# Linear attention and a max-out layer on one core: softmax row sums kept and checked on the chip, with a second program part behind a branch

## The chip, the core and the metric

The kernel runs on one core of one Trainium2 chip. The metric is the device time of one execution in microseconds. The kernel before takes 320.04 us (median of 3 runs, 319.87 to 320.14).

## What is computed

Attention with projected keys and values (Linformer), then a layer that takes the elementwise maximum of two products:

```python
k_proj = einsum('ks,bhsd->bhkd', E, k)          # 1024 positions down to 64
v_proj = einsum('ks,bhsd->bhkd', F, v)
scores = q @ k_proj.T / sqrt(64)
scores = scores - max(scores, axis=-1)
attn = exp(scores); attn = attn / (sum(attn, axis=-1) + 1e-9)
x = (attn @ v_proj)  as [8192 tokens, 512]      # 8 batches x 1024 positions, 8 heads x 64
out = maximum(x @ w1, x @ w2) @ w_out           # 512 -> 1024 -> 512, fp32 out
```

The inputs are fp32: q, k and v of 8 x 8 x 1024 x 64, E and F of 64 x 1024, w1 and w2 of 512 x 1024, w_out of 1024 x 512.

## The kernel before

All matmuls are in fp16 with fp32 sums. The kernel does not subtract the row maximum: with a softmax the result is the same as long as no exponential and no sum leaves its number range. The exponentials of the scores are written as fp16 (`ex_sb`). Their row sums are made on TensorE by a product with a matrix of ones (`sums_into`, L353), so each sum stands in 32 partitions at once. ScalarE takes the logarithm of the sums (L382 or L448) into `ld_sb` and then exp(-x) in place (L386, `step_inv`, or L452, `invert`), which gives the inverse sums. VectorE multiplies the attention's output by them (L401, L456).

The max-out layer is rewritten: max(a, b) = b + relu(a - b), so that one product with w1 - w2 (`wd_sb`), a relu and a product with w_out are needed, and a product of x with w2 @ w_out (`m_sb`). These are done by a Strassen-Winograd scheme of 7 products for 8 (`up_steps`, `down_steps`, products p1 to p7), in 16 units of 512 tokens: two for each batch. The matmuls of the up products are at L702, those of the down products at L794. In every unit VectorE adds the parts (L717, L720 for relu, L824 for the output), and ScalarE copies banks out (L676) or makes the output's fourth part (L898). A bank "X" goes on being added to after its first copy: p6 continues on p1's bank.

The order of work is written out by hand. `slots` is one list of steps for all engines: of unit n the down products are slots ("P", n, p, i); between them stand the up products of unit n + 1, slots ("U", n, h, i), where h is the half and i the product; ("G", n, h) is the place where a group of the attention of a later batch (scores, sums, values) is put. `at_slot(key, step)` hangs a step behind a slot. Each engine runs its part of that list in order. So does SP, whose queue carries the first loads, the DMA transposes of q (L317, `step_qt_dma`) and of the projected k (L291), and the stores of the output (L810). GpSimd issues the other loads; for batches 4 and up a small copy on GpSimd (`step_gate`, L297) waits for the transposes before the next batch is loaded.

Buffers come from pools: `soft` (5 buffers) holds `ex_sb` and `ld_sb`; batch 0 takes `ld_sb` from `ppool` instead. `opool` has 14 output tiles; the stores of units 0 and 1 are held back and put into later slots (`held`). Two PSUM tiles named `att_ps` serve the attention. The last unit's last product is cut small (L886, L892), so that the last stores are small. Line L1161 is the end of the program: SP waits for every DMA, and barriers close it.

Of the kernel before, what the change touches and what calls it, by code (L numbers as in the profile page):

```python
# [1 line left out]

# [5 lines left out]

FP32 = mybir.dt.float32
FP16 = mybir.dt.float16  # L10
LN_EXP_SET = 6
ACTF = mybir.ActivationFunctionType
ALU = mybir.AluOpType

# [2 lines left out]
def kernel(  # L17
# [12 lines left out]
    nc = tc.nc  # L30

    B, H, S, D = q.shape
    KP = E.shape[0]
    DM = moe_w1.shape[0]
    DF = moe_w1.shape[1]
    NC = S // 128
# [5 lines left out]

    scale = 1.0 / float(D) ** 0.5

    const = ctx.enter_context(tc.tile_pool(name="const", bufs=1))
    kvq = ctx.enter_context(tc.tile_pool(name="kvq", bufs=4))
    proj = ctx.enter_context(tc.tile_pool(name="proj", bufs=2))
# [1 line left out]
    xpool = ctx.enter_context(tc.tile_pool(name="xpool", bufs=2))  # L49
    gpool = ctx.enter_context(tc.tile_pool(name="gpool", bufs=2))  # L50
    soft = ctx.enter_context(tc.tile_pool(name="soft", bufs=5))
    opool = ctx.enter_context(tc.tile_pool(name="opool", bufs=14))
    ppool = ctx.enter_context(tc.tile_pool(name="ppool", bufs=4))
    ps = ctx.enter_context(tc.tile_pool(name="ps", bufs=1, space=bass.MemoryType.PSUM))

# [9 lines left out]
    def att_banks(dtype=FP32):  # L65
        return ps.tile(
            [128, 2, 512 if dtype == FP32 else 1024], dtype, tag="att", bufs=2, name="att_ps"
        )
# [25 lines left out]
    def alloc(t, n):  # L94
        t[n] = kvq.tile([128, H, NC, D], FP16, tag="kvq", name=f"{n}_sb")

# [22 lines left out]
    w1_sb = big(1).rearrange("p (r f) -> p r f", r=NDC)  # L119
    w2_sb = big(2).rearrange("p (r f) -> p r f", r=NDC)  # L120
    wo_sb = const.tile([128, NFB, DM], FP16, tag="wo", name="wo_sb")
    for g in range(2):
        for w_sb, w in ((w2_sb, moe_w2), (w1_sb, moe_w1)):
            nc.gpsimd.dma_start(
                out=w_sb.rearrange("p (g z) f -> p g z f", z=2)[:, g, :, 0:256],
                in_=w.rearrange("(g p z) f -> p g z f", p=128, z=2)[:, g, :, 0:256],
            )
    for w_sb, w, f0, f1 in (
# [27 lines left out]
    eft = [const.tile([128, NC, KP], FP16, tag=f"eft{i}", name=f"eft{i}") for i in range(2)]  # L156
# [167 lines left out]
    W = HALF // 2  # L324
    Z = D // 2

    def score(t, g, j, banks):
        for h in range(2):
            for o in range(2):
                for e in range(2):  # L330
                    head = 4 * g + 2 * h + e
                    for s in range(2):
                        pos = D * (o ^ e) + s * Z
                        nc.tensor.matmul(  # L334
                            out=banks[e][pos : pos + Z, h * W : (h + 1) * W],
                            lhsT=kpt_of(t, head, o)[:, s * Z : (s + 1) * Z],
                            rhs=t["qt"][o * D : (o + 1) * D, head, j * W : (j + 1) * W],
                            start=True, stop=True,
                        )
        t["ex", g, j] = soft.tile([128, 2, HALF], FP16, tag="soft", name="ex_sb")  # L340
# [24 lines left out]

    def x_out(t, g, j):
        return t["xt"][:, 2 * g : 2 * g + 2, :, j * W : (j + 1) * W]


    def step_sc(t, g, j):  # L370
        sc_ps = att_banks()
        t["ps", g, j] = sc_ps
        score(t, g, j, [sc_ps[:, e, :] for e in range(2)])
        nc.scalar.activation(out=t["ex", g, j], in_=sc_ps, func=ACTF.Exp, scale=scale)  # L374

    def step_dn(t, g, j):
# [4 lines left out]
        t["ld", g, j] = ld  # L381
        nc.scalar.activation(out=t["ld", g, j], in_=dn_ps, func=ACTF.Ln)  # L382

    def step_inv(t, g, j):
        ld = t["ld", g, j]
        nc.scalar.activation(out=ld, in_=ld, func=ACTF.Exp, scale=-1.0)  # L386

    def step_at(t, g, j, att=False, between=None):
        if "xt" not in t:
            new_xt(t)  # L390
        ld = t.pop(("ld", g, j))
        if att:
            both = att_banks()
            at_ps = [both[:, o, :] for o in range(2)]
        else:
            at_ps = [mm_bank() for _ in range(2)]
        values_into(t, g, j, at_ps)
        for o in range(2):
            if o and between is not None:
                between()  # L400
            nc.vector.tensor_tensor(  # L401
                out=x_out(t, g, j)[:, :, o, :],
                in0=at_ps[o].rearrange("q (z n) -> q z n", z=2),
                in1=ld[:, o, None, :].broadcast_to([128, 2, W]),
                op=ALU.mult,
            )
# [18 lines left out]
    def scores(t, g, j, banks):  # L425
        for e in t["first"]:
            nc.scalar.activation(  # L427
                out=t["ex", g, j][:, e, :], in_=banks[e], func=ACTF.Exp, scale=scale
            )
# [7 lines left out]
    def step_da(t, g, j, between, ln_later):  # L437
        if "xt" not in t:
            new_xt(t)
        dn_ps = att_banks()[:, :, 0:W]  # L440
        at_ps = att_banks()
        sums_into(t, g, j, dn_ps)
        values_into(t, g, j, [at_ps[:, o, :] for o in range(2)])
        between()
        ld = soft.tile([128, 2, W], FP32, tag="soft", name="ld_sb")

        def ln():
            nc.scalar.activation(out=ld, in_=dn_ps, func=ACTF.Ln)  # L448
            return invert

        def invert():
            nc.scalar.activation(out=ld, in_=ld, func=ACTF.Exp, scale=-1.0)  # L452
            return finish

        def finish():
            nc.vector.tensor_tensor(  # L456
                out=x_out(t, g, j).rearrange("q z o n -> q o z n"),
                in0=at_ps.rearrange("q o (z n) -> q o z n", z=2),
                in1=ld[:, :, None, :].broadcast_to([128, 2, 2, W]),
                op=ALU.mult,  # L460
            )

        return ln if ln_later else ln()
# [503 lines left out]
    f = lambda s, *a: lambda: s(tiles[0], *a)  # L967
# [56 lines left out]
    def at_slot(key, s, *a):  # L1024
        steps.setdefault(key, []).append(lambda: s(*a))
# [14 lines left out]
    for n, x in enumerate((  # L1040
# [4 lines left out]
        for name in x.split():  # L1045
# [6 lines left out]
            else:  # L1052
                g, j = int(name[2]), int(name[3])
# [22 lines left out]
    for b in range(3, B):  # L1076
        t = tiles[b]
        n = 2 * b - 3
# [13 lines left out]
    for i, (new, old) in enumerate(zip([*groups[1:], none], groups)):  # L1092
        n, h = divmod(i + 2, 2)
# [9 lines left out]
    for n, (b, o) in enumerate(units):  # L1103
# [14 lines left out]
        if n:  # L1118
            end = ("U", n - 1, 1, 6) if n > 1 else ("P", 0, 6, 1)
            m = 0 if n == last else 2  # L1120
            one = end if n == 1 else ("G", n, 0) if n in kv_units else ("P", n, 0, 0)
            for key, i in (end, 0), (one, 1), (("P", n, 1, m), 2), (("P", n, 2, m), 3):
                at_slot(key, sums_g, u, (i,))

    pending = []
    for key, slot in slots:
        r = slot()
        pending = [g for g in [r, *(f() for f in pending)] if g is not None]
        for s in steps.pop(key, ()):
            r = s()  # L1130
# [2 lines left out]
    assert not pending  # L1133
    assert not steps
    assert not held


# [28 lines left out]
```

## Time and profile before

| | |
|---|---|
| median of 3 runs | 320.04 us (319.87 to 320.14) |
| profiled execution, span | 318.0 us |
| outside the span, against the median | 2.0 us |
| instructions in the span | 9177 |
| TensorE busy | 312.1 us |
| VectorE busy | 240.4 us |
| ScalarE busy | 206.1 us |
| GpSimd busy | 40.0 us |
| DMA | 53.41 MB in 76424 packets |

The profile is of one execution on the chip. Its own time is the span, from the first to the last instruction, and the time around it that belongs to the launch. Engines are named PE (TensorE matmul), PEld (TensorE weight load), DVE (VectorE), ACT (ScalarE), POOL (GpSimd) and SP (SyncE); a q behind a name means its sequencer, which issues DMAs and waits for semaphores. In a timeline the columns are the start in us, the length in us, the engine, the line, the operation with its tiles and shapes, and in brackets the idle time before and what ended it. In a list by line the numbers are count, shortest/median/longest duration in ns, and first and last start.

### The profile page before, as it was taken

Reading aid. Unit: us, or ns where it says so; the run is one execution under the profiler, and the core shown is the slowest. Engines: PE = TensorE matmul, PEld = TensorE weight load, DVE = VectorE, ACT = ScalarE, POOL = GpSimd, SP = SyncE. Lnnn points to the kernel's source line nnn. Section 1 sums busy time; section 2 is a strip of 40 time slices with the busy share of each in tenths; the row PEclk is TensorE's granted clock in tenths of the full one; section 3 lists DMA queues with packets and bytes.
Section 4 is the critical chain, followed back from the end, with each engine's and each line's share of the span. In section 5 each row is a group of like instructions: output and inputs, shape, how many; then the busy total and the mean of one; then the engine's idle time right before and its main releaser. Section 6 shows DMA issues by size and latency. Waiting matters only on the chain.

```text
span 318.0 us, 9177 instructions
## 1 busy us (share of the span) xinstructions
PE 312.1 (98%) x3920; PEld 253.5 (80%) x3920; DVE 240.4 (76%) x437; ACT 206.1 (65%) x372; POOL 40.0 (13%) x63
## 2 busy tenths in 40 slices
PE   8989999999999999999999999999999999999996
PEld 3555588788887888788887888788887888888885
DVE  2366888877969696996969696996969696969683
ACT  2476843777776777477776778477776777765541
POOL 8269002003000300030000400040000000000000
DMA  7999999999969899899989999989969131303124
GB/s 184 203 200 197 204 206 203 207 180 157 205 119 197 152 217 245 212 182 172 237 196 213 165 200 244 221 154 179 235 142 207 45 102 35 101 33 102 35 99 132
DMA packets 76424, 53.41 MB, mean 168 GB/s; under 512 B 29536, under 2 KB 76000, under 8 KB 76384
## 3 DMA queue, kind: packets, MB, share of 16 engines
q0 software_dynamic: 30688, 28.05, 56.4%
q1 hardware_dynamic: 45408, 24.58, 32.2%
q8 instruction: 30, 0.49, 0.6%
q10 hardware_dynamic: 288, 0.20, 0.2%
q14 instruction: 10, 0.08, 0.1%
HBM read 57.15 MB, written 16.78 MB: 233 GB/s over the span
## 4 chain that ended last, share of the span: by engine, by line
PE 92%; DMA 4%; POOL 1%; ACT 1%; DVE 0%; issue 0%; POOLq 0%; DVEq 0%
PE mm_ps L794 47%; PE mm_ps L702 27%; PE mm_ps L481 4%; DMA v_sb<-in_v_dram 4%; PE att_ps L346 3%; PE mm_ps L189 3%; PE mm_ps L334 2%; PE mm_ps L590 2%; PE att_ps L231 1%; PE mm_ps L305 1%; POOL k_sb L102 0%; POOL q_sb L102 0%; ACT ld_sb L382 0%; ACT ex_sb L374 0%; DVE o_sb L892 0%; PE att_ps L513 0%
## 5 line engine op out<-in xcount | busy, mean ns | idle before, releaser
L676 ACT COPY p_sb<-mm_ps 128x512 f32<-128x512 f32 x179 | 101.8, 592 | 49.4 <-PE mm_ps L702 27.6
L794 PEld LDWEIGHTS <-big 128*128 128x128 f16 x768 | 73.6, 98 | 11.8 <-issue 3.6
L794 PE MATMUL mm_ps<-T_sb,big 128*128 128x256 f16 x576 | 76.9, 273 | 0.0
L717 DVE TENSOR_TENSOR gt_sb<-mm_ps,p_sb 128x512 f16<-128x512 f32 x56 | 38.5, 688 | 43.9 <-PE mm_ps L702 43.6
L702 PE MATMUL mm_ps<-big,big 128*128 128x256 f16 x336 | 50.4, 273 | 0.0
L702 PEld LDWEIGHTS <-big 128*128 128x128 f16 x448 | 43.8, 98 | 5.1
L794 PE MATMUL mm_ps<-wo_sb,gt_sb 128*128 128x256 f16 x256 | 42.6, 273 | 0.0
L794 PEld LDWEIGHTS <-gt_sb 128*128 128x128 f16 x376 | 35.7, 98 | 6.7 <-issue 2.7
L427 ACT ACTIVATE ex_sb<-mm_ps 128x512 f16<-128x512 f32 x50 | 27.2, 596 | 18.0 <-PE mm_ps L334 12.3
L702 PEld LDWEIGHTS <-wd_sb 128*128 128x128 f16 x336 | 32.9, 98 | 3.8
L702 PE MATMUL mm_ps<-xt_sb,wd_sb 128*128 128x256 f16 x224 | 32.8, 273 | 0.0
L456 DVE TENSOR_TENSOR xt_sb<-att_ps,ld_sb 128x1024 f16<-128x1024 f32 x26 | 31.7, 1219 | 0.2
L794 PE MATMUL mm_ps<-m_sb,xt_sb 128*128 128x256 f16 x128 | 24.4, 273 | 0.0
L824 DVE TENSOR_TENSOR o_sb<-mm_ps,p_sb 128x512 f32<-128x512 f32 x32 | 21.9, 683 | 2.8 <-ACT p_sb L853 2.0
L297 POOL COPY junk<-qt_sb 1x1 f16<-1x1 f16 x6 | 1.5, 246 | 175.1 <-DMA qt_sb<-q_sb 175.1
L720 DVE TENSOR_SCALAR gt_sb<-gt_sb 128x512 f16<-128x512 f16 (+1 forms) x60 | 21.5, 359 | 2.1
L662 DVE TENSOR_TENSOR big<-gt_sb 128x1024 f16<-128x1024 f16 x32 | 21.9, 683 | 0.0
L794 PE MATMUL mm_ps<-wo_sb,big 128*128 128x256 f16 x128 | 21.5, 273 | 0.0
L763 ACT ACTIVATE gt_sb<-mm_ps 128x512 f16<-128x512 f32 x28 | 16.8, 601 | 5.7 <-PE mm_ps L702 5.7
L794 PE MATMUL mm_ps<-T_sb,gt_sb 128*128 128x256 f16 x120 | 20.3, 273 | 0.0
L794 PEld LDWEIGHTS <-xt_sb 128*128 128x128 f16 x188 | 18.3, 98 | 2.3 <-issue 0.2
L717 DVE TENSOR_TENSOR gt_sb<-p_sb 128x512 f16<-128x512 f32 x28 | 19.1, 682 | 0.6 <-ACT p_sb L676 0.6
(113 smaller groups left out, 432.3 us busy)
## 6 DMA issues: line engine op xcount, KB each, us to landing
out_dram<-o_sb SPq DMA_DIRECT2D x62, 256.0 KB, 2.7
k_sb<-in_k_dram POOLq DMA_DIRECT2D x7, 1024.0 KB, 10.6
v_sb<-in_v_dram POOLq DMA_DIRECT2D x7, 1024.0 KB, 16.6
q_sb<-in_q_dram POOLq DMA_DIRECT2D x5, 1024.0 KB, 23.5
q_sb<-in_q_dram POOLq DMA_DIRECT2D x6, 512.0 KB, 16.2
big<-in_moe_w_dram POOLq DMA_DIRECT2D x12, 128.0 KB, 6.6
v_sb<-in_v_dram POOLq DMA_DIRECT2D x4, 256.0 KB, 13.5
wo_sb<-in_moe_w_out_dram POOLq DMA_DIRECT2D x1, 1024.0 KB, 10.8
```

The lines of the kernel that those rows point to most:

```text
L189: nc.tensor.matmul(out=kv_ps[r * KP : (r + 1) * KP, h * D : (h + nh) * D], lhsT=eft[i][:, c, :], rhs=t[w][:, h0 + h : h0 + h + nh, c, :], ...
L427: nc.scalar.activation(out=t["ex", g, j][:, e, :], in_=banks[e], func=ACTF.Exp, scale=scale)
L456: nc.vector.tensor_tensor(out=x_out(t, g, j).rearrange("q z o n -> q o z n"), in0=at_ps.rearrange("q o (z n) -> q o z n", z=2), in1=ld[:, ...
L481: nc.tensor.matmul(out=h_ps, lhsT=wd_sb[:, r, fb * 128 : (fb + 1) * 128], rhs=t["xt"][:, r, :, j * W : (j + 1) * W], start=(r == 0), stop= ...
L662: nc.vector.tensor_tensor(out=S(i), in0=S(0) if x is None else x, in1=y(), op=op)
L676: copy(out=x, in_=bank)
L702: nc.tensor.matmul(out=bank[:, m * W : (m + 1) * W], lhsT=w_[:, n_, (2 * d + m) * 128 : (2 * d + m + 1) * 128], rhs=a[:, n_, :], start=(n ...
L717: nc.vector.tensor_tensor(out=c_blk(j, c), in0=two(x), in1=two(y), op=ALU.add)
L720: nc.vector.tensor_scalar_max(ap, ap, 0.0)
L763: nc.scalar.activation(out=out, in_=in_, func=ACTF.Relu)
L794: nc.tensor.matmul(out=bank[i][:, 0:CH] if two_banks else bank[:, i * CH : (i + 1) * CH], lhsT=a(c)[:, i * 128 : (i + 1) * 128], rhs=w_(c) ...
L824: nc.vector.tensor_tensor(out=o_sb, in0=two(x), in1=two(y), op=ALU.add)
```

## The change

Each inverse (`step_inv`, `invert`) is followed by a small DMA on SP's queue: 4 of the 128 rows (one out of every 32 equal ones), 512 values each, go into a tile `checked` of 128 x 512. There are 32 such DMAs, and after the last one `checked` holds every row's inverse sum. In the half ("U", 14, 1) VectorE takes the largest and the smallest value of each partition (on the bits as integers, which orders positive floats and also catches what is not a number), compares them with 1/16 and 1/60000, and writes 0, 1 or 2 to `bad`. A matmul with ones adds `bad` over the partitions, and ScalarE copies one element to `flag`. At the end of the program every engine loads `flag` and branches: where it is not zero, `tile_shifted` computes the whole output again in fp32, with row maxima subtracted. The code marks a place for a branch hint in the same half. The output pool has 13 tiles in place of 14, which makes room for the new tiles.

```diff
+SUM_MIN, SUM_MAX = 16.0, 60000.0
...
+    guard = ctx.enter_context(tc.tile_pool(name="guard", bufs=1))
+    flag = guard.tile([1, 1], I32, name="flag")
+    outer, ctx = ctx, ExitStack()
...
-    opool = ctx.enter_context(tc.tile_pool(name="opool", bufs=14))
+    opool = ctx.enter_context(tc.tile_pool(name="opool", bufs=13))
...
+    checked = const.tile([128, 2 * W], FP32, name="checked")
+    n_checked = [0]
+
+    def check(inv):
+        rows = checked[4 * n_checked[0] : 4 * n_checked[0] + 4, :]
+        n_checked[0] += 1
+        nc.sync.dma_start(
+            out=rows, in_=inv.rearrange("(a z) o w -> a z (o w)", z=Z)[:, 0, :]
+        )
+
+    def step_guard():
+        bits = checked.bitcast(I32)
+        ends = const.tile([128, 4], FP32, name="ends")
+        bad = ends.bitcast(FP16)[:, 4:5]
+        as_bits = lambda x: float(struct.unpack("i", struct.pack("f", x))[0])
+        for i, op in enumerate((ALU.max, ALU.min)):
+            nc.vector.tensor_reduce(
+                out=ends[:, i : i + 1], in_=bits, op=op, axis=mybir.AxisListType.X
+            )
+        nc.vector.tensor_scalar(
+            out=ends[:, 0:1], in0=ends[:, 0:1], scalar1=as_bits(1.0 / SUM_MIN), scalar2=None,
+            op0=ALU.is_gt, op1=ALU.bypass,
+        )
+        nc.vector.tensor_scalar(
+            out=bad, in0=ends[:, 1:2], scalar1=as_bits(1.0 / SUM_MAX), scalar2=ends[:, 0:1],
+            op0=ALU.is_lt, op1=ALU.add,
+        )
+        return bad
+
+    def step_flag(bad):
+        n_ps = att_banks()[:, 0, 0:1]
+        nc.tensor.matmul(out=n_ps, lhsT=ones16[:, 0:128], rhs=bad, start=True, stop=True)
+        nc.scalar.copy(out=flag, in_=n_ps[0:1, :])
+
     def step_inv(t, g, j):
         ld = t["ld", g, j]
         nc.scalar.activation(out=ld, in_=ld, func=ACTF.Exp, scale=-1.0)
+        check(ld)
...
         def invert():
             nc.scalar.activation(out=ld, in_=ld, func=ACTF.Exp, scale=-1.0)
+            check(ld)
             return finish
...
+    bad = []
+    at_slot(("U", last - 1, 1, 0), lambda: bad.append(step_guard()))
+    at_slot(("U", last - 1, 1, 1), lambda: step_flag(bad[0]))
+    at_slot(("U", last - 1, 1, 1), lambda: tc.mark_branch_hint_location(
+        "shifted", "LikelyTaken", mybir.ALL_ENGINES))
...
+    ctx.close()
+
+    with tc.If(nc.values_load(flag, min_val=0, max_val=256, ...), preferred_fallthrough_block=True, label="shifted"):
+        tile_shifted(tc, q, k, v, E, F, moe_w1, moe_w2, moe_w_out, out)
+
+
+@with_exitstack
+def tile_shifted(ctx, tc, q, k, v, E, F, w1, w2, w_out, out):
...
+    for b in range(B):
+        body(b)
```

`tile_shifted` is unrolled: for each of the 8 batches it loads k, v and q in fp32, projects them, and for each 128 positions makes the scores, subtracts the row maximum, and does the softmax, the two up products, their maximum and the down product, without overlap between steps. `preferred_fallthrough_block=True` puts its instructions right behind the branch, so that the branch is taken, over them, where the flag is zero.

More of the change, by code (lines that the diff above doesn't have):

```diff
@@ L1 @@
+import struct
 from contextlib import ExitStack
@@ L10 @@
 FP16 = mybir.dt.float16
+I32 = mybir.dt.int32
 LN_EXP_SET = 6
+SUM_MIN, SUM_MAX = 16.0, 60000.0
 ACTF = mybir.ActivationFunctionType
@@ L382, in step_dn @@
         nc.scalar.activation(out=t["ld", g, j], in_=dn_ps, func=ACTF.Ln)
+    checked = const.tile([128, 2 * W], FP32, name="checked")
[7 more added lines that the diff above has]
+    def step_guard():
+        assert n_checked[0] == B * H * S // (2 * W) // 4
+        bits = checked.bitcast(I32)
[19 more added lines that the diff above has]
+        nc.scalar.copy(out=flag, in_=n_ps[0:1, :])
     def step_inv(t, g, j):
@@ L1135, with bank, turned, body @@
     assert not held
+    ctx.close()
+    with tc.If(nc.values_load(flag, min_val=0, max_val=256, skip_runtime_bounds_check_because="it is only compared with zero"), preferred_fallthrough_block=True, label="shifted"):
+        tile_shifted(tc, q, k, v, E, F, moe_w1, moe_w2, moe_w_out, out)
+@with_exitstack
+def tile_shifted(ctx, tc, q, k, v, E, F, w1, w2, w_out, out):
+    nc = tc.nc
+    B, H, S, D = q.shape
+    KP, DM, DF = E.shape[0], *w1.shape
+    P = 128
+    NC, NX, NG = S // P, DM // P, DF // P
+    AX = mybir.AxisListType.X
+    once = ctx.enter_context(tc.tile_pool(name="once", bufs=1))
+    work = ctx.enter_context(tc.tile_pool(name="work", bufs=1))
+    psum = ctx.enter_context(tc.tile_pool(name="psum", bufs=1, space=bass.MemoryType.PSUM))
+    ident = once.tile([P, P], FP32, name="ident_s")
+    make_identity(nc, ident)
+    def bank(n):
+        return psum.tile([P, 512], FP32, tag=f"b{n}", name=f"b{n}")
+    def turned(dst, blocks, n):
+        cols, rows = blocks[0].shape
+        for i0 in range(0, len(blocks), 512 // cols):
+            part = blocks[i0 : i0 + 512 // cols]
+            ps = bank(n)
+            for i, x in enumerate(part):
+                nc.tensor.transpose(
+                    out=ps[0:rows, i * cols : (i + 1) * cols], in_=x, identity=ident[0:cols, 0:cols]
+                )
+            nc.vector.tensor_copy(
+                out=dst[0:rows, i0 * cols : (i0 + len(part)) * cols], in_=ps[0:rows, 0 : len(part) * cols]
+            )
+    w1_sb, w2_sb = (once.tile([P, NX, DF], FP32, name=f"w{i}_s") for i in (1, 2))
+    wo_sb = once.tile([P, NG, DM], FP32, name="wo_s")
+    for sb, w in (w1_sb, w1), (w2_sb, w2), (wo_sb, w_out):
+        nc.gpsimd.dma_start(out=sb, in_=w.rearrange("(r p) f -> p r f", p=P))
+    ef = once.tile([KP, 2, S], FP32, name="ef_s")
+    eft = once.tile([P, 2, NC * KP], FP32, name="eft_s")
+    for i, w in enumerate((E, F)):
+        nc.gpsimd.dma_start(out=ef[:, i], in_=w)
+        turned(eft[:, i], [ef[:, i, c * P : (c + 1) * P] for c in range(NC)], 0)
+    def body(b):
+        x_in = {}
+        for n, src in (("k", k), ("v", v), ("q", q)):
+            x_in[n] = work.tile([P, NC, H, D], FP32, tag="in" if n != "q" else "q", name=f"{n}_s")
+            for h in range(H):
+                nc.gpsimd.dma_start(
+                    out=x_in[n][:, :, h, :], in_=src[b, h].rearrange("(c p) d -> p c d", p=P)
+                )
+            if n == "q":
+                break
+            proj = work.tile([KP, H * D], FP32, tag=f"{n}p", name=f"{n}p_s")
+            ps = bank(1)
+            for c in range(NC):
+                nc.tensor.matmul(
+                    out=ps[0:KP, :], lhsT=eft[:, "kv".index(n), c * KP : (c + 1) * KP],
+                    rhs=x_in[n][:, c].rearrange("p h d -> p (h d)"),
+                    start=(c == 0), stop=(c == NC - 1),
+                )
+            nc.vector.tensor_copy(out=proj, in_=ps[0:KP, :])
+            x_in[n + "p"] = proj
+        kpt = work.tile([D, H * KP], FP32, tag="kpt", name="kpt_s")
+        turned(kpt, [x_in["kp"][:, h * D : (h + 1) * D] for h in range(H)], 0)
+        for c in range(NC):
+            qt = work.tile([D, H * P], FP32, tag="qt", name="qt_s")
+            turned(qt, [x_in["q"][:, c, h, :] for h in range(H)], 0)
+            sc_ps = bank(1)
+            for h in range(H):
+                nc.tensor.matmul(
+                    out=sc_ps[:, h * KP : (h + 1) * KP], lhsT=qt[:, h * P : (h + 1) * P],
+                    rhs=kpt[:, h * KP : (h + 1) * KP], start=True, stop=True,
+                )
+            sc = work.tile([P, H, KP], FP32, tag="sc", name="sc_s")
+            top = work.tile([P, H], FP32, tag="top", name="top_s")
+            per = lambda a: a[:, :, None].broadcast_to([P, H, KP])
+            nc.vector.tensor_copy(out=sc.rearrange("p h k -> p (h k)"), in_=sc_ps)
+            nc.vector.tensor_reduce(out=top, in_=sc, op=ALU.max, axis=AX)
+            nc.vector.tensor_tensor(out=sc, in0=sc, in1=per(top), op=ALU.subtract)
+            nc.scalar.activation(out=sc, in_=sc, func=ACTF.Exp, scale=1.0 / float(D) ** 0.5)
+            nc.vector.tensor_reduce(out=top, in_=sc, op=ALU.add, axis=AX)
+            nc.vector.tensor_scalar(
+                out=top, in0=top, scalar1=1e-9, scalar2=None, op0=ALU.add, op1=ALU.bypass
+            )
+            nc.vector.reciprocal(out=top, in_=top)
+            nc.vector.tensor_tensor(out=sc, in0=sc, in1=per(top), op=ALU.mult)
+            at = work.tile([KP, H * P], FP32, tag="at", name="at_s")
+            turned(at, [sc[:, h, :] for h in range(H)], 0)
+            x_ps = bank(1)
+            for h in range(H):
+                nc.tensor.matmul(
+                    out=x_ps[:, h * D : (h + 1) * D], lhsT=at[:, h * P : (h + 1) * P],
+                    rhs=x_in["vp"][:, h * D : (h + 1) * D], start=True, stop=True,
+                )
+            x = work.tile([P, DM], FP32, tag="x", name="x_s")
+            nc.vector.tensor_copy(out=x, in_=x_ps)
+            xt = work.tile([P, DM], FP32, tag="xt", name="xt_s")
+            turned(xt, [x[:, r * P : (r + 1) * P] for r in range(NX)], 0)
+            g = work.tile([P, DF], FP32, tag="g", name="g_s")
+            for f in range(0, DF, 512):
+                for i, w in enumerate((w1_sb, w2_sb)):
+                    ps = bank(2 + i)
+                    for r in range(NX):
+                        nc.tensor.matmul(
+                            out=ps, lhsT=xt[:, r * P : (r + 1) * P], rhs=w[:, r, f : f + 512],
+                            start=(r == 0), stop=(r == NX - 1),
+                        )
+                    if i == 0:
+                        nc.vector.tensor_copy(out=g[:, f : f + 512], in_=ps)
+                    else:
+                        nc.vector.tensor_tensor(
+                            out=g[:, f : f + 512], in0=g[:, f : f + 512], in1=ps, op=ALU.max
+                        )
+            gt = work.tile([P, DF], FP32, tag="gt", name="gt_s")
+            turned(gt, [g[:, r * P : (r + 1) * P] for r in range(NG)], 0)
+            o_ps = bank(1)
+            for r in range(NG):
+                nc.tensor.matmul(
+                    out=o_ps, lhsT=gt[:, r * P : (r + 1) * P], rhs=wo_sb[:, r, :],
+                    start=(r == 0), stop=(r == NG - 1),
+                )
+            o_sb = work.tile([P, DM], FP32, tag="o", name="o_s")
+            nc.vector.tensor_copy(out=o_sb, in_=o_ps)
+            nc.gpsimd.dma_start(
+                out=out.rearrange("(n c p) m -> n c p m", c=NC, p=P)[b, c], in_=o_sb
+            )
+    for b in range(B):
+        body(b)
```

## The prediction

> **What bounds the kernel now.** I read the page first: how busy each engine is, the instruction queues, and the shares of the chain that ended last.
>
> ```profile
> span 318.0 us, 9177 instructions
> PE 312.1 (98%) x3920; PEld 253.5 (80%) x3920; DVE 240.4 (76%) x437; ACT 206.1 (65%) x372; POOL 40.0 (13%) x63
> q8 instruction: 30, 0.49, 0.6%
> q14 instruction: 10, 0.08, 0.1%
> PE 92%; DMA 4%; POOL 1%; ACT 1%; DVE 0%; issue 0%; POOLq 0%; DVEq 0%
> ```
>
> TensorE is the bound: it is busy 98% of the span, and the chain is TensorE for 92%. So work on another engine costs nothing unless TensorE, or the end of the program, comes to wait for it. The two queue rows are the program itself being read: 30 blocks of 0.49 MB / 30 = 16 KB, which at 7,840 TensorE instructions (3920 + 3920) is TensorE's own stream at about 62 bytes each, and 10 blocks of 8 KB for other engines.
>
> Next, the timeline where the change puts its new VectorE work and its one new matmul (unit 14, second half), VectorE and TensorE together.
>
> ```profile
> 298.45 0.29 DVE L720 TENSOR_SCALAR gt_sb<-gt_sb 128x512 f16<-128x512 f16 x1
> 300.73 0.60 PE L702 MATMUL mm_ps<-xt_sb,wd_sb 128*128 128x256 f16 x4
> 301.17 0.38 PE L794 MATMUL mm_ps<-m_sb,big 128*128 128x256 f16 x2
> 301.44 0.69 DVE L717 TENSOR_TENSOR gt_sb<-mm_ps,p_sb 128x512 f16<-128x512 f32 x1 [2.70 <-PE mm_ps L702]
> 302.30 0.59 ACT L676 COPY p_sb<-mm_ps 128x512 f32<-128x512 f32 x1 [1.17 <-PE mm_ps L702]
> ```
>
> VectorE ends the second relu of p3 at 298.74 and stands idle 2.70 us until p2's product; ScalarE stands idle 1.17 us just behind. Matmuls start 0.109 us apart (four in 0.44).
>
> Then the tail: the last links of the chain, and what the closing line L1161 does on each queue.
>
> ```profile
> 305.70 7.86 PE mm_ps L794 x72
> 313.56 0.67 PE mm_ps L886 x6
> 314.31 0.90 DVE o_sb L892 x3
> ...
> L1161 SPq EVENT_SEMAPHORE  x11: 17/28/28, 315.6 to 317.9; - x11
> L1161 SPq DRAIN  x3: 7/7/13, 317.1 to 317.4; - x3
> L1161 PEldq DRAIN  x2: 13/615/1217, 313.7 to 317.5; - x2
> L1161 DVEq DRAIN  x2: 19/174/330, 314.9 to 317.5; - x2
> L1161 ACTq DRAIN  x2: 8/79/150, 315.3 to 317.4; - x2
> ```
>
> The sequencers come to the end at 313.7 (TensorE, running ahead of its matmuls), 314.9 (VectorE), 315.3 (ScalarE) and 315.6 (SP). All then stand until 317.1, when the last store (issued at 315.24) has landed and SP may drain. So there is room of 3.4, 2.2, 1.8 and 1.5 us in which an end of program can hide. The last 0.9 us, to 318.0, are the closing barriers.
>
> Last, the early stretch, where SP's queue is tight.
>
> ```profile
> 59.76 0.63 ACT L386 ACTIVATE ld_sb<-ld_sb 128x512 f32<-128x512 f32 x1
> 66.01 6.18 SPq L317 DMA_TRANSPOSE qt_sb<-q_sb  x2
> 72.88 1.09 ACT L427 ACTIVATE ex_sb<-mm_ps 128x512 f16<-128x512 f32 x2 [0.65 <-PE mm_ps L334]
> ```
>
> SP waits 63.5 us for q of batch 2 before the first transpose (the queue's own waits), and the inverse sums of batch 1 are made in that wait.
>
> **The changed order.** I compared the order of instructions of both kernels on every engine. TensorE, VectorE, ScalarE and GpSimd keep their order. They gain only: a weight load and a 128x1 matmul; two reductions and two 128x1 operations; one 1x1 copy; and on every engine a prefetch hint, a register load and a branch. The hint stands first in the program, not in unit 14 where the code marks it. SP gains 32 DMAs, four for a batch, in between stores and transposes.
>
> **32 row copies (8 KB each).** SP issues a DMA in 0.34 to 0.58 us, so 32 cost some 15 us of a queue that waits 163.7 us for VectorE's sums alone. Queued behind each waiting copy are the stores and transposes made after it, but the inverse it waits for precedes theirs, so they lose at most 0.6 us. Stores have a median landing of 2.7 us; a buffer of ex or ld is taken again two groups (some 18 us) later. The bytes are 0.26 of 53.4 MB. The one tight place is 66 to 73 us: copies 5 and 6 (batch 1) now sit between the two transposes. The first transpose is not moved; it ends at about 66.0 + 3.1 = 69.1, copy 5 is issued by 69.7 and, landing behind the transpose's data (GpSimd saw those at 71.68), is there at about 72. The exponential that takes its buffer starts at 72.88. So 0 now, 0.9 us of cover, and if that is gone up to 1 us. The second transpose goes 1.2 us later; its scores come at 80.63 and the loads behind it (batch 3) are used from 97 us on: hidden. 0 in the sum.
>
> **Extra waits.** ScalarE gets 18 more semaphore instructions, VectorE 6, at 17 to 28 ns: 0.6 us beside TensorE's work: 0.
>
> **Output buffers 14 to 13.** Followed through, the closest reuse now is the 19th tile on the store of the 6th issue, some 510 program positions earlier; at 9115 positions in 318 us that is 17 us against a landing of 2.7 us plus up to 6.2 us behind two transposes: 0.
>
> **Reductions and flag.** A 128x512 f32 operation takes 0.68 us (683 ns, L824), a small one at most 0.23 (227 ns, L153): 2 x 0.68 + 2 x 0.23 = 1.8 us, from 298.74 to 300.6, inside the 2.70 us and ahead of the flag's matmul at 301.17. Were a reduction as slow as the 1.22 us of L456, it would be 2.9 us, and TensorE would wait 0.5 us. I take 0. The 1x1 copy (0.22 us, L239) fits into ScalarE's 1.17 us. On TensorE the new pair costs 0.055 (the spacing of the 128-column pairs in the tail, six in 0.33 us) to 0.109 us: +0.1.
>
> **Hint at the start.** A sequencer instruction: 0.02 to 0.5 us (a semaphore row, a DMA issue); on the path, as the start waits for loads that SP and GpSimd issue: +0.1.
>
> **The end.** Every engine now loads the flag into a register, compares and jumps over the second part. No trace of before shows a register load: it lies between a semaphore instruction (0.03) and a whole DMA (1.7 us, the 64 KB store); I take 0.6, near the 0.58 of SP's first DMA issue, also one request to memory by a sequencer. [...] Branch and jump: 0.1.
>
> What decides is whether the target is there. It lies 1 instruction beyond the branch for SP, 136 for ScalarE (8.5 KB, about the next block), 1503 for VectorE (94 KB) and 4711 for TensorE (0.29 MB, 18 blocks). The rows show blocks streamed one after another, so I expect VectorE and TensorE to have the second part's blocks, not the target's. A fetch costs the block's own transfer, 0.6% x 16 x 318 / 30 = 1.0 us for TensorE and 0.1% x 16 x 318 / 10 = 0.5 us for the others, plus the fixed part of a small DMA, 1.7 us as the 64 KB store: 2.7 and 2.2. Bounds: 1.0 (the transfer alone) and 3.7 us (the 256 KB load of E).
> - SP: 315.6 + 0.7, then its semaphores, still before 317.1.
> - VectorE: 314.9 + 0.7 + 2.2 + 0.1 = 317.9, 0.8 past 317.1.
> - TensorE: 313.7 + 0.7 + 2.7 + 0.1 = 317.2.
> - ScalarE: if it too misses, 318.3, 1.2 past.
> - GpSimd ends its work at 246.4 and branches once the flag is written, at about 302: nothing.
>
> I take VectorE's 0.8 us plus 0.1 for a part of ScalarE's: +0.9. [...]
>
> **Sum.** 0.1 + 0.1 + 0.9 = +1.1 us on a span of 318.0, so 319.1. The median of the runs, 320.04, is 2.0 above the span, and nothing in the change touches what lies around it: 321.1 us. The runs spread by 0.27 us; 0.2%, or 0.64 us, is about what a measurement of this kernel can tell from no change.
>
> **Rivals.**
> 1. Not slower: the hint works. The target's block is fetched ahead, VectorE is through at 315.7 and SP at 316.6 with its dozen semaphores (0.3 us), both before 317.1. Left are the 0.2 us of pair and hint: 320.2. The point is a fetch of 317.1 - 315.7 = 1.4 us; below it nothing shows. For it: the instruction is made for this branch, and so far ahead that there is time. Against: it stands some 315 us and up to 30 blocks before its branch, so what it fetches may long be overwritten.
> 2. The early copies: copy 5 lands after 72.9, ScalarE's exponential and the copies behind it slip, and TensorE, which adds to a bank only three products (1.3 us) after the one that is copied out, waits. Price up to 1 us there, besides the 1.1: 322.1. Against: 0.9 us of cover.
> 3. The long fetch: 3.7 us on ScalarE and VectorE, 315.3 + 0.7 + 3.7 + 0.1 = 319.8, 2.7 us past: 322.9.
> 4. The check misfires and the second part runs. Sums of 64 exponentials of small scores lie near 64, in range, so the flag is zero. If not, thousands of fp32 matmuls would at least double the time.
>
> **How the numbers follow.** Forecast 0.50, rival 1 0.33, rival 2 0.06, rival 3 0.08, rival 4 0.01; 0.02 for a schedule that happens to fall better. Short fetches (under 1.8 us) leave a tenth of the forecast's chance within 0.2%, and a fifth of rival 1's ends above it. Slower: 0.45 + 0.07 + 0.06 + 0.08 + 0.01 = 0.67; same 0.05 + 0.26 = 0.31; faster 0.02. The range reaches from rival 1 to rival 3: 320.1 to 322.9.
>
> **What would show it.** Right: TensorE's chain unchanged to about 314.5, VectorE's hole filled from 298.7, no wait at the 128x1 matmul, and VectorE's and perhaps ScalarE's first instruction behind the branch 2 us or more after it, with SP waiting for that and not for the store. Wrong: the closing drain still at about 1.5 us after SP's last issue; or TensorE idle near 73 or 301 us; or a late start.

## The result, and the profile after

The changed kernel takes 322.13 us (median of 4 runs, 321.98 to 322.76), the kernel before beside it 320.06 us (4 runs, 319.87 to 320.14). The ratio is 1.0066, with a 95% interval of 1.0051 to 1.008: slower by 2.07 us, where 1.1 had been forecast.

The page of after, the lines that answer to those of before:

```profile
span 320.4 us, 9299 instructions
PE 311.9 (97%) x3921; PEld 253.6 (79%) x3921; DVE 241.2 (75%) x441; ACT 206.2 (64%) x373; POOL 40.3 (13%) x63
q8 instruction: 31, 0.51, 0.6%
q14 instruction: 13, 0.11, 0.1%
PE 91%; DMA 4%; POOL 1%; ACT 1%; issue 1%; DVE 0%; POOLq 0%; DVEq 0%
```

TensorE is busy for the same time. The two queue rows are the program itself being read: one more block of TensorE (q8, 31 for 30) and three more of other engines (q14, 13 for 10). That is the first hint of where to look.

The place of the check, in the timeline of after, VectorE, TensorE and ScalarE:

```profile
298.93 0.29 DVE L763 TENSOR_SCALAR gt_sb<-gt_sb 128x512 f16<-128x512 f16 x1
299.23 1.28 DVE L407 TENSOR_REDUCE ends<-checked 128x1 f32<-128x512 int32 x2
301.64 0.17 PE L422 MATMUL att_ps<-ends,ones 128*128 128x1 f16 x1
301.88 0.15 ACT L423 CAST flag<-att_ps 1x1 int32<-1x1 f32 x1 [0.27 <-PE att_ps L422]
301.91 0.69 DVE L760 TENSOR_TENSOR gt_sb<-mm_ps,p_sb 128x512 f16<-128x512 f32 x1 [1.09 <-PE att_ps L422]
```

The hole that VectorE had here is filled, and 1.09 us of it is left. No wait stands in front of the 128x1 matmul. The row of VectorE names that matmul as its releaser, but the product it adds ended in the same moment, and the length of the idle time adds up as before: 2.70 less the 1.6 us of new work.

The end of the chain, then the jump (L1187: register load and branch on every engine), then the closing line, which is L1345 now:

```profile
306.20 7.86 PE mm_ps L837 x72
314.06 0.67 PE mm_ps L929 x6
314.81 0.91 DVE o_sb L935 x3
```
```profile
L1187 PEldq TENSOR_LOAD <-flag x1: 805/805/805, 314.2 to 314.2; - x1
L1187 PEldq COMPARE_BRANCH  x1: 385/385/385, 315.1 to 315.1; - x1
L1187 DVEq TENSOR_LOAD <-flag x1: 574/574/574, 315.4 to 315.4; - x1
L1187 DVEq COMPARE_BRANCH  x1: 84/84/84, 316.1 to 316.1; - x1
L1187 ACTq COMPARE_BRANCH  x1: 68/68/68, 316.6 to 316.6; - x1
L1187 SPq COMPARE_BRANCH  x1: 72/72/72, 316.8 to 316.8; - x1
```
```profile
L1345 SPq EVENT_SEMAPHORE  x14: 17/28/28, 317.0 to 320.4; - x14
L1345 SPq DRAIN  x3: 7/7/13, 319.6 to 319.9; - x3
L1345 PEldq DRAIN  x2: 8/8/8, 315.7 to 319.9; - x2
L1345 DVEq DRAIN  x2: 10/14/17, 316.8 to 319.9; - x2
L1345 ACTq DRAIN  x2: 8/8/8, 317.2 to 319.9; - x2
```

All engines are past the jump and at the closing line at 315.7 (TensorE), 316.8 (VectorE), 317.2 (ScalarE) and 317.0 us (SP). Nobody stands at a branch. Yet SP drains only at 319.6, where it drained at 317.1 before. What SP waits for is the stores: its last one is issued at 315.74 and is complete at 319.41, 3.67 us later (the completion is the last count on the store's semaphore in the trace). In the trace of before it is issued at 315.24 and complete at 316.98, 1.74 us later. So the 2.49 us by which the span grew (320.44 less 317.95) are 0.50 us of a chain that ends later (314.81 against 314.31 for VectorE's last link), 1.93 us of a store that lands later, and 0.06 us in the closing barriers.

The landing itself can be taken apart. Each store is counted in 16 parts. Of the last three, 15 parts are there at 317.16, 317.34 and 317.50, and one part of each at 318.94, 319.21 and 319.41. The DMA view of two windows shows what moved then (queue q1 is SP's, q10 ScalarE's, q8 and q14 the program's own). In the trace of before, 315.9 to 317.7 us has no block:

```profile
q1 hardware_dynamic: 201, 0.11, 20.3%
q10 hardware_dynamic: 144, 0.07, 13.1%
```

In the trace of after, the same window has three:

```profile
DMA packets 459, 0.31 MB, mean 175 GB/s; under 512 B 61, under 2 KB 456, under 8 KB 456
q8 instruction: 1, 0.02, 5.2%
q14 instruction: 2, 0.02, 3.5%
```

And then, in the trace of after, 317.72 to 319.6 us:

```profile
DMA packets 26, 0.02 MB, mean 8 GB/s; under 512 B 3, under 2 KB 26, under 8 KB 26
q1 hardware_dynamic: 17, 0.01, 3.1%
q10 hardware_dynamic: 9, 0.00, 0.7%
```

The second window holds 26 packets, 9 of them on q10, which is a sixteenth of the 144 packets of ScalarE's store: it looks as if one DMA engine out of 16 is late. In the first window lie one block of 16 KB for TensorE (from 316.17 us, 1.51 us long) and two of 8 KB for other engines (from 317.28 and 317.68, 0.53 and 0.47 us). So a new explanation offers itself, which the forecast did not have: **the jump makes the sequencers read program at the very moment at which the last stores move, and the blocks stand in front of one engine's share of them.** The profile does not name the DMA engine of a packet; that block and late packets share one is inferred from the sixteenth and from the times. The times are close: the first packet of the late share starts at 317.66 us, just as TensorE's block ends (316.17 and 1.51, so 317.68), and it is the same in the runs below (317.61 and 317.62 in e14_block_away, 317.71 and 317.73 in e9_near_hint).

### The profile page after: what moved, and what is told of

It is laid out like the page before. It is cut to its first block, busy times and chain, and to the rows that moved or that the text cites. A ratio compares the mean times of both kernels' runs of the same rounds, so it can differ in the third digit from the quotient of the medians.

```text
span 320.4 us, 9299 instructions
## 1 busy us (share of the span) xinstructions
PE 311.9 (97%) x3921; PEld 253.6 (79%) x3921; DVE 241.2 (75%) x441; ACT 206.2 (64%) x373; POOL 40.3 (13%) x63
## 4 chain that ended last, share of the span: by engine, by line
PE 91%; DMA 4%; POOL 1%; ACT 1%; issue 1%; DVE 0%; POOLq 0%; DVEq 0%
PE mm_ps L837 46%; PE mm_ps L745 27%; PE mm_ps L524 4%; DMA v_sb<-in_v_dram 4%; PE att_ps L352 3%; PE mm_ps L195 3%; PE mm_ps L340 2%; PE mm_ps L633 2%; PE att_ps L237 1%; PE mm_ps L311 1%; POOL q_sb L108 0%; ACT ld_sb L388 0%; ACT ex_sb L380 0%; DVE o_sb L935 0%; PE att_ps L556 0%
```

## The experiments

Each figure is the median, with the ratio to the kernel before run beside it. "Block" is the start of TensorE's program block near the end, "landed" the last part of the last store, "drain" SP's first drain at the closing line, all from the profiled execution.

| kernel | median us | ratio, 95% | block | landed | drain |
|---|---|---|---|---|---|
| before | 320.06 | | none | 316.98 | 317.12 |
| after | 322.13 | 1.0066 (1.0051 to 1.008) | 316.17 | 319.41 | 319.55 |
| e1_no_branch | 320.0 | 0.9992 (0.9974 to 1.001) | none | 317.40 | 317.54 |
| e3_no_hint | 321.72 | 1.0054 (1.0035 to 1.0073) | 316.3, 319.5 | 318.79 | 319.00 |
| e2_near | 322.12 | 1.0065 (1.0042 to 1.0088) | 316.2 | 318.81 | 318.95 |
| e8_near_plain | 320.51 | 1.0011 (1.0002 to 1.0021) | none | 317.36 | 317.66 |
| e9_near_hint | 322.49 | 1.0077 (1.006 to 1.0094) | 316.02 | 319.35 | 319.49 |
| e6_early_load | 321.7 | 1.0055 (1.0039 to 1.0071) | 315.7 | 318.56 | 318.70 |
| e10_early_plain | 321.79 | 1.0056 (1.0036 to 1.0076) | 315.1, 318.4 | 318.42 | 318.56 |
| e7_late_jump | 321.19 | 1.0028 (1.0013 to 1.0043) | 318.8 | 317.51 | 318.46 |
| e11_hint_te | 322.13 | 1.0071 (1.0054 to 1.0088) | 315.92 | 318.94 | 319.08 |
| e12_hint_others | 322.19 | 1.0071 (1.0054 to 1.0088) | 316.18 | 319.15 | 319.30 |
| e13_hint_two | 322.22 | 1.0089 (1.0052 to 1.0126) | 318.6 | 321.80 | 321.94 |
| e14_block_away | 322.18 | 1.0069 (1.0052 to 1.0086) | 316.01 | 319.25 | 319.40 |

### The check without the jump: e1_no_branch

The hint, the register load, the branch and the second part are left out; copies, reductions and flag stay.

```diff
-    at_slot(("U", last - 1, 1, 1), lambda: tc.mark_branch_hint_location(
-        "shifted", "LikelyTaken", mybir.ALL_ENGINES))
...
-    with tc.If(nc.values_load(flag, ...), ...):
-        tile_shifted(tc, q, k, v, E, F, moe_w1, moe_w2, moe_w_out, out)
```

> The change without its end: the sums are still kept, reduced and turned into the flag, but nothing loads the flag, there is no hint, no branch and no second part. Theory A (after the jump the sequencers fetch the program block behind the target, and that fetch stands in front of one DMA engine's sixteenth of the last stores): the last stores land within 1.8 us of their issue as before, 320.1 to 320.6 us. Theory B (register load, compare, jump and a longer list of closing waits make the end longer): the same 320.1 to 320.6. Theory C (0.4 us of the loss come from the hint at the start): no shift of TensorE at 40 us, 320.1; if the shift stays, it is the copies or chance, 320.5.

It is as fast as before. Everything that the check does on the chip is hidden, and the whole loss belongs to what this run leaves out: the hint, the register load, the jump and the second part. Its last VectorE link starts at 314.71 us, 0.40 later than in the trace of before, without a loss in the median. So most of the 0.50 us by which the chain of after is shifted is likely the chance of single profiled executions, and not the change. The shift is there within the first 40 us, where TensorE still waits for the first loads.

### Without the hint: e3_no_hint

```diff
-    at_slot(("U", last - 1, 1, 1), lambda: tc.mark_branch_hint_location(
-        "shifted", "LikelyTaken", mybir.ALL_ENGINES))
```

> The whole change without the branch hint. Theory A: the hint had the target block there in time; without it TensorE, VectorE and ScalarE wait 1 to 2.7 us for a block after the compare, and the block behind follows, so SP's closing wait ends 1 to 3 us later than with the hint: 322.5 to 325 us. Theory B, or a hint without effect: 322.1 us. Theory C: 0.4 us less from the start in either case.

It is not slower than with the hint: 321.72 us, below the 322.5 to 325 us of Theory A. The 0.4 us less than with the hint are Theory C's figure, but the first matmul starts only 0.10 us sooner (1.45 against 1.55 us), and the intervals of the two kernels overlap. The long wait comes, though, at TensorE's branch:

```profile
L1185 PEldq COMPARE_BRANCH  x1: 4189/4189/4189, 314.6 to 314.6; - x1
```

4.19 us for a branch that takes 0.385 us with the hint. So with the hint TensorE does not stand at its branch; but without it TensorE is through at 318.8 us, just when the last store lands, which is late here too (318.79).

### A short second part: e2_near, e8_near_plain, e9_near_hint

First the second part was cut to one DMA (128 rows of the output over 128 others; it does not compute the output where the flag is set), with the hint kept:

```diff
-        tile_shifted(tc, q, k, v, E, F, moe_w1, moe_w2, moe_w_out, out)
+        nc.gpsimd.dma_start(out=out[0:128], in_=out[128:256])
```

> The whole change, with hint, register load, compare and jump on all engines, but the second part is one DMA, so that the target lies one to three instructions beyond the branch. Theory A: no block is fetched at the end, the last stores land in time, 320.1 to 320.6 us. Theory B: the same end as with the long second part, 321.6 to 322.1 us.

The time is the one of Theory B, and a block is read (at 316.2 us), which Theory A did not expect. But this does not decide: the schedule put SP's last store behind the branch (issued at 316.96 for 315.74 us), which alone makes the end later. In the next pair the DMA touches all rows, so that every store stays ahead of the branch as in the changed kernel; one is without the hint, one with it:

```diff
+        nc.gpsimd.dma_start(out=out[0:4096], in_=out[4096:8192])
```

> As the near second part before, but that part now copies half of the output onto the other half, so that all stores stay ahead of the branch, and there is no hint. Theory A (the instruction blocks that are fetched after the jump stand in front of the last stores on one DMA engine): the branch stays in a block that is there, nothing is fetched, the last stores land 1.8 us after issue: 320.0 to 320.4 us. Theory B (load, compare, jumps and the longer list of closing waits cost by themselves): 321.5 to 322.1.

> The same with the hint. Theory A, with the hint replacing the next block by the target's: one 16 KB block for TensorE is still fetched right after its jump, though the target is two instructions away, and the last stores of one DMA engine land 1 to 1.5 us late: 321.0 to 321.8 us. A hint that does nothing for a near target: 320.0 to 320.4. Theory B: 321.5 to 322.1, as without hint.

Without the hint (L1185 is the jump, L1212 the closing line):

```profile
L1185 PEldq TENSOR_LOAD <-flag x1: 796/796/796, 314.1 to 314.1; - x1
L1185 PEldq COMPARE_BRANCH  x1: 215/215/215, 315.0 to 315.0; - x1
L1212 SPq DRAIN  x3: 7/7/13, 317.7 to 318.0; - x3
```

With it (L1214 is the closing line), and its DMA window 315.9 to 317.7 us:

```profile
L1187 PEldq COMPARE_BRANCH  x1: 385/385/385, 315.0 to 315.0; - x1
L1214 SPq DRAIN  x3: 7/7/13, 319.5 to 319.8; - x3
q8 instruction: 1, 0.02, 5.9%
q14 instruction: 1, 0.01, 1.8%
```

The first is 0.1 us above Theory A's range and a full 1 us below Theory B's: register loads, branches and jumps together cost 0.48 us (320.51 against 320.03; the ratio is 1.0011, 1.0002 to 1.0021). The second takes 322.49 us, 0.7 more than Theory A expected of it. So the rest of the loss, some 2 us, comes with the block, and the block came here with the hint alone. I first took it for the hint's doing.

### When the jump comes: e6_early_load, e10_early_plain, e7_late_jump

In all three the register load stands in slot ("P", last, 1, 0), under the last unit's work.

```diff
+    loaded = []
+    at_slot(("P", last, 1, 0), lambda: loaded.append(nc.values_load(flag, ...)))
...
-    with tc.If(nc.values_load(flag, ...), ...):
+    with tc.If(loaded[0], preferred_fallthrough_block=True, label="shifted"):
```

> The whole change, but each engine loads the flag into its register in the last unit, behind p2, and not behind its last work. Theory A: the jumps and so the fetches come 0.6 to 0.8 us sooner, before the smallest stores are under way, 321.0 to 321.7 us. Theory B: the load's 0.6 us leaves the end, 321.5 us, with the last landing as late against its issue as before the edit.

The block is read 0.44 us earlier than in the changed kernel, and the median is 0.43 us lower, though the two intervals overlap. Both theories allow this median; the landing speaks for Theory A, as it comes 2.94 us after the last store's issue at 315.62, for 3.67 in the changed kernel. In the second the hint is left out as well:

> The whole second part, flag loaded in the last unit, no hint. Theory A: TensorE's target block is fetched once, 0.8 us sooner than without the early load, mostly ahead of the last stores; VectorE's and ScalarE's blocks 0.6 us sooner: 320.9 to 321.5 us. If the fetches cost by the wait of the jumping engine and not by the stores: 321.3 to 321.7.

Its jump (L1188) on TensorE and VectorE:

```profile
L1188 PEldq COMPARE_BRANCH  x1: 3689/3689/3689, 314.0 to 314.0; - x1
L1188 DVEq EVENT_SEMAPHORE  x1: 21/21/21, 318.3 to 318.3; - x1
```

TensorE stands 3.7 us at its branch, and a block is read meanwhile (from 315.1 us). That it waits for its target is the author's reading. VectorE's branch ends at 315.3 and its next instruction comes at 318.3: 3 us. ScalarE, whose target is 136 instructions away, goes on 0.4 us later (316.1). The median of 321.79 us is above both expected ranges.

Which store is the first to have a sixteenth more than 1 us late moves with the block. Where the block is read at 315.11 (e10_early_plain), it is a store whose other 15 parts are there at 315.93 and whose last part comes at 317.43. With the block at 315.73 (e6_early_load) it is the next one, 316.36 and 317.83. With the block at 316.17 (the changed kernel) both of these have landed whole by 316.50, and the first late one is at 317.16 and 318.94. So the lateness follows the block and not the store.

In the third kernel (with the hint) the jumps of VectorE, TensorE and ScalarE are put behind the landing of the last store, by a write of VectorE into the last output tile and a product and a copy that read it:

```diff
...
+    cell = final[0][:, 1, CH - 1 : CH]
+    nc.vector.memset(cell, 0.0)
+    nc.tensor.matmul(out=att_banks()[:, 0, 0:1], lhsT=ones16[:, 0:128],
+                     rhs=cell.bitcast(FP16)[:, 0:1], start=True, stop=True)
+    nc.scalar.copy(out=final[0][:, 1, CH - 2 : CH - 1], in_=cell)
```

> The whole second part with hint, flag loaded in the last unit, and a write into the last output tile after its store, with one matmul and one copy that read it, so that VectorE, TensorE and ScalarE jump only once the last store has landed. Theory A: no fetch is under way while the stores are, so they land 1.7 us after issue again, and only compare, jump and semaphores come behind, 0.5 to 0.9 us: 320.6 to 321.1 us, though the jumps come 2 us later than with the early load. Theory B, or a jump that costs by its own length: slower than the early load's 321.7, 322.0 to 323.5 us.

The jumps (L1198) and SP's drain (L1356):

```profile
L1198 DVEq COMPARE_BRANCH  x1: 90/90/90, 317.6 to 317.6; - x1
L1198 PEldq COMPARE_BRANCH  x1: 383/383/383, 317.7 to 317.7; - x1
L1356 SPq DRAIN  x3: 7/7/13, 318.5 to 318.8; - x3
```

TensorE jumps 2.6 us later than in the changed kernel, and the kernel ends earlier by 0.9 us (321.19 against 322.13). The block is read at 318.8, when no store is under way, and the stores land in their usual 1.76 us (315.75 to 317.51). This is the plainest evidence for the collision: the same jump, the same blocks, only not at the same time as the stores. Since the flag is loaded early here too, the fair comparison is e6_early_load, and against that the later jump is still 0.5 us faster (321.19 against 321.70). It is 0.1 us above the range that Theory A gave.

### Whose hint, and whose block: e11_hint_te, e12_hint_others, e13_hint_two

Short second part as in e9, the hint for TensorE alone, and for the other four alone; and the full second part with the hint for TensorE and VectorE.

```diff
-        "shifted", "LikelyTaken", mybir.ALL_ENGINES))
+        "shifted", "LikelyTaken", [mybir.EngineType.PE]))        # e11
+        "shifted", "LikelyTaken", [e for e in mybir.ALL_ENGINES if e != mybir.EngineType.PE]))  # e12
+        "shifted", "LikelyTaken", [mybir.EngineType.PE, mybir.EngineType.DVE]))  # e13
```

> The kernel with the short second part (one DMA of rows 4096 to 8191 over rows 0 to 4095, so it doesn't compute the output where the flag is set) and the hint for TensorE alone. Theory A (the block behind a hinted target is read on one DMA engine that also carries a sixteenth of the last stores): TensorE's 16 KB block is still read at about 316, 1.5 to 1.7 us long, no 8 KB block behind it, so the last part of the last store lands about 0.5 us earlier than with all five hints (319.35 there): about 318.8, and the median is 321.7 to 322.2. Rival D (the hints delay the end by something else, each engine's hint its own share): about 0.4 us for each engine hinted, 320.9.

> The same with the hint for the four engines other than TensorE (again with the second part cut to one DMA). Theory A: no 16 KB block near 316, one or two 8 KB blocks at about 317, 0.5 us each, which arrive behind most of the stores: the last landing at 317.5 to 318.3, median 320.6 to 321.4. Rival D (a share for each engine): four fifths of the loss, about 322.1.

> The full second part, hint for TensorE and VectorE alone (the two whose target lies many blocks away). Theory A: the 16 KB block at about 316 and VectorE's 8 KB block still stand before the last store; ScalarE's is read or not by its own order. Last landing 318.9 to 319.4, median 321.8 to 322.2, within 0.3 us of the changed kernel (322.13). Rival D: two fifths of the hints' loss, about 321.2.

All three lose what the changed kernel loses, so a share of the loss for each hinted engine is ruled out: it would have given 320.9 for e11 and 321.2 for e13. (Two of the five runs of e13 take 324.74 and 324.95 us, the others 321.96 to 322.22. Its profile is of one of the long ones, shifted by some 2.5 us from its first loads on; its tail is as long as the others'.) But e12 missed, and it taught the most: TensorE has no hint there, it executes the same operations as in e8_near_plain, and its block is read nevertheless, 1.0 us after the start of its branch:

```profile
L1187 PEldq COMPARE_BRANCH  x1: 350/350/350, 315.2 to 315.2; - x1
q8 instruction: 1, 0.02, 4.7%
```

Likewise e11 reads an 8 KB block 1.2 us after the start of VectorE's branch (VectorE's by its time: the changed kernel and e9 have one 1.2 us after that branch too), and VectorE has no hint there; this block, too, was not expected. So it is not the engine's own hint instruction that makes it read the block. TensorE's branch takes 350 ns where it took 215 ns in e8, so the jump itself differs; the place of the target is a guess at why.

### A target 13 KB further on, no hint: e14_block_away

```diff
+        nc.gpsimd.dma_start(out=out[0:4096], in_=out[4096:8192])
+        matmuls(tc)
...
+    nc.gpsimd.memset(a, 1.0)
+    for _ in range(100):
+        nc.tensor.matmul(out=p, lhsT=a, rhs=a, start=True, stop=True)
```

> No hint on any engine; the second part is one DMA of rows 4096 to 8191 over rows 0 to 4095 and 204 instructions of TensorE (100 products of a tile of ones), so it doesn't compute the output where the flag is set. TensorE's target is then 13 KB away, most likely in the block behind the branch's; the other engines' targets are 1 to 9 instructions away. Theory A2 (what counts is that a jump enters another block: TensorE then reads the block behind it, on the DMA engine that carries a sixteenth of the last stores; hints do the same, on all engines at once): a 16 KB block at about 316 and no 8 KB block at 317, no stall at TensorE's branch as its target was read ahead, last landing 318.5 to 319, median 321.5 to 322.2. Theory H (only hints cause it): as the short second part without a hint, all landings by 317.4, median 320.5. Theory M (the target isn't there): TensorE's branch takes 3 to 4 us, its drain comes at 318.5 or later, median 321 to 322.

The jump (L1185), the closing line (L1224), and the DMA window 315.9 to 317.7 us:

```profile
L1185 PEldq COMPARE_BRANCH  x1: 350/350/350, 314.9 to 314.9; - x1
L1224 SPq DRAIN  x3: 7/7/13, 319.4 to 319.7; - x3
L1224 PEldq DRAIN  x2: 8/8/8, 315.5 to 319.8; - x2
q1 hardware_dynamic: 271, 0.19, 33.9%
q10 hardware_dynamic: 138, 0.06, 12.8%
q8 instruction: 1, 0.02, 5.6%
```

No hint, no stall at the branch (350 ns, and TensorE is at the closing line at 315.5), no block of another engine, and the whole loss: 322.18 us. The 204 instructions of TensorE that are jumped over are never run; at the 62 bytes each that q8's 0.49 MB give over 7,840 TensorE instructions in the trace of before, they are an estimated 13 KB. What is executed is that of e8_near_plain but for a semaphore instruction more on TensorE and GpSimd and a few semaphores that SP waits for; TensorE lands 13 KB further on, and the last landing moves from 317.36 to 319.25 (318.5 to 319 was expected). Together with the later jump (e7_late_jump) this shows the cause: **a jump over 13 KB of program is enough to make TensorE's sequencer read one more block (31 on q8, 30 in e8_near_plain), though it goes on 0.5 us after its branch begins, and that read of 16 KB beside the last stores costs 1.7 us** (322.18 less 320.51). The 8 KB blocks of the other engines add little: the changed kernel has two of them and lands 0.16 us later, with a last issue 0.18 us later.

TensorE's blocks come on q8 while it works: 31 of them in the changed kernel, with TensorE busy 97% of the span.

The packets of e14_block_away also show why the late share ends so long after the block. The block ends at 317.62, and from 317.33 to 317.60 no packet starts at all. One starts at 317.61, and from 317.72 to 319.6 us the DMA view has:

```profile
DMA packets 26, 0.02 MB, mean 8 GB/s; under 512 B 3, under 2 KB 26, under 8 KB 26
q1 hardware_dynamic: 17, 0.01, 3.0%
q10 hardware_dynamic: 9, 0.00, 0.7%
```

These 27 are a sixteenth of each of the three stores, 9 packets each, one behind the other until 318.72. The first six take 0.09 to 0.14 us, where such a packet usually takes 0.05. The three parts are counted about 0.5 us behind their last packets, at 318.85, 319.05 and 319.25.

What stays open is where the blocks of the program lie: no run shows it. That 13 KB count because the jump enters another block, and that the mark of a hint puts the target of every engine into another block (which would explain e9, e11 and e12), are guesses; the equal 350 ns of e12 and e14 speak for the second.

No guarded version came out ahead of the kernel before. The best with the full second part is e7_late_jump, 1.0028 (1.0013 to 1.0043).

## Why the prediction was right, and where it was not

The direction was right and the time lies in the range, but the forecast's main term was right in nothing but its sign. That the time fell into the range is luck.

- **TensorE's order, the 32 copies, the extra waits, 13 buffers, the early transposes: 0 each.** Right: e1_no_branch has them all and is as fast as before. The copies take 496 to 869 ns each on SP, somewhat more than the 0.34 to 0.58 us assumed, and copies 5 and 6 stand between the transposes as said, without a wait of TensorE behind them. Rival 2 falls, though its price, 322.1 us, happens to be what was measured.
- **Reductions and flag: +0.1.** The reductions take 0.68 us each, as assumed (1.28 from the first one's start to the second's end), the two small operations 0.14 and 0.22, all inside the hole. The pair costs TensorE at most 0.03 us. The place was right, the cost smaller.
- **Hint at the start: +0.1.** 50 to 56 ns on each engine, and the first work of the engines starts about 0.1 us later. Right.
- **Register load 0.6, branch and jump 0.1.** 493 to 805 ns, and 65 to 84 ns (TensorE 385). Right but for TensorE's branch.
- **The end: VectorE and TensorE lack their target, +0.9 us.** This step failed: no run shows the 0.9 us. With the hint no engine stands at its branch (TensorE's takes 0.385 us and VectorE goes on 0.5 us behind its own); rival 1 had that right, against the argument that a hint so early would be overwritten. Without a hint the stall is there, and longer than the 2.7 and 2.2 us worked out: 3.7 us for TensorE and 3 us for VectorE in e10_early_plain, and 4.2 us for TensorE in e3_no_hint, beyond the upper bound of 3.7.
- **Rival 1's conclusion**, that nothing shows once the fetch is in time, failed too, and for the reason for which the forecast's sum was short. Both treated the closing wait to 317.1 us as a fixed cover under which a jump could hide, because the last store has been issued by then. The cover is made of a transfer, and the program's block delayed a sixteenth of that transfer. The term to put there was not 0.9 us of a stall on VectorE but 1.9 us on the last store's landing (3.67 against 1.74 us). Loads and jumps, which the forecast counted only on the way to VectorE's miss, cost 0.48 us by themselves where no block is read (e8_near_plain); in the changed kernel they lie under the late landing, as SP is at the closing line at 317.0.
- **What would show it wrong** had been written down: the closing drain still about 1.5 us after SP's last issue, or an idle TensorE, or a late start. None of the three came; the drain is 3.8 us after the start of SP's last issue, where it was 1.9 in the trace of before. But the sign that was to show the forecast right, an engine late behind its branch, did not come either. The total fell within the range by a mechanism that was on neither list.

## What to carry to other kernels

The branch at the end of this kernel was paid for in what its jump made the sequencer read (1.7 us, e14_block_away against e8_near_plain) more than in loading the flag and branching (0.48 us, e8_near_plain). So if nothing but stores is in flight there, ask which blocks of program will move beside them, and count the blocks by queue in that window. Keep what is jumped over so short that no further block is read, and then without a hint (e8_near_plain lost 0.5 us; with the hint, e9_near_hint lost 2.5, and 13 KB were already too far), or let the jump fall where no transfer decides the end (e7_late_jump). A wait that looks like free cover is only free for work that does not use what is waited for: here the last store landed 3.67 us after its issue, for 1.74 us before.

## What the runs showed of the hardware that was not expected

- The read of a program block delayed data: 16 KB for TensorE took 1.4 to 1.7 us beside the last stores (the changed kernel, e9, e12 and e14; mostly 0.9 to 1.1 us in mid-kernel), and one sixteenth of each of the stores behind it landed late, by 1.8 to 1.9 us in the changed kernel.
- A jump over 13 KB cost 1.7 us against e8 without a stall at the branch (e14): TensorE's branch takes 350 ns (215 ns in e8, with the target next to it), and a block is read 1.1 us after its start. An 8 KB block follows 1.2 us after the start of VectorE's branch in the changed kernel, e9, e11 and e12.
- A hint for some engines made others without one read a block too (TensorE in e12, VectorE in e11); the reason is open.
- Without a hint, and with the full second part, TensorE's branch took 3.7 to 4.2 us (e10, e3), and VectorE went on about 3 us after its own; with the hint it was 0.385 and 0.5 us (the changed kernel).
